# Attention heads in a four-layer network: one pool of six PSUM banks for both score products and the values, and masked scores written in place

## The chip, the cores and the metric

One core of a Trainium2 chip runs the whole program. The metric is the device time of one execution in microseconds, here the median of three runs. The core has a matrix engine (PE, with its weight loads shown as PEld), a vector engine (DVE), an activation engine (ACT), a general engine (POOL) and the queue that issues the DMA transfers (SP). Each engine works through its own instructions in program order, and semaphores hold it where it needs another engine's result. PE writes its products to PSUM, which this kernel uses as eight banks of 512 float32 columns on 128 partitions.

## The reference

The input is x, 2048 rows of 640 values. Four layers follow, attention, Fourier, attention, Fourier, each adding to x:

```python
def _A_ref(x, wqkv, wo):
    H = 32; Dh = D // H; W = 256
    qkv = (lambda x, *d: x.transpose(*d))((x @ wqkv).reshape(B, S, 3, H, Dh), 2, 0, 3, 1, 4)
    q, k, v = qkv[0], qkv[1], qkv[2]
    scores = jnp.einsum("bhqd,bhkd->bhqk", q, k) * (Dh ** -0.5)
    mask = (idx[:, None] - idx[None, :] >= 0) & (idx[:, None] - idx[None, :] < W)
    p = _softmax(jnp.where(mask[None, None], scores, -1e9), axis=-1)
    o = jnp.einsum("bhqk,bhkd->bhqd", p, v)
    return (lambda x, *d: x.transpose(*d))(o, 0, 2, 1, 3).reshape(B, S, D) @ wo
...
x = x + _A_ref(_layernorm(x, axis=-1), A_wqkv, A_wo)
x = x + _B_ref(_layernorm(x, axis=-1), B_dft_seq_re, B_dft_seq_im, B_dft_hid_re, B_dft_hid_im)
x = x + _A_ref(_layernorm(x, axis=-1), A_wqkv, A_wo)
x = x + _B_ref(_layernorm(x, axis=-1), B_dft_seq_re, B_dft_seq_im, B_dft_hid_re, B_dft_hid_im)
```

Each of the 32 heads has 20 values a row, and a row sees itself and the 255 rows before it. `_B_ref` is the real part of a two-dimensional Fourier transform, done as products with given matrices; the change doesn't touch it.

## The kernel before

Products of float32 values are made of three products each: an operand is split into a high and a low part (`split`), and high x high, high x low and low x high are summed. The scores put the three side by side along the 60 rows of one matmul.

In an attention layer the heads are taken four at a time, eight groups called quads, with 16 blocks of 128 rows each. `heads` runs over 128 steps, one for each block of each quad, after ten steps of lead. A step t does several things that belong to different blocks, in two halves z = 0 and z = 1 with two heads each:

- `t_pair` (L571): the transposed scores of block t, keys on the partitions, up to 384 query columns, for two heads into two banks. The heads lie on different rows of PE, so the two matmuls run side by side. `t_exp` (L580) takes both banks through the exponential on ACT in one instruction of 768 columns and writes them to SBUF (`pt`). `t_mask` (L586, L590) clears on POOL what the window leaves out.
- `s_head` (L542, L547): the scores of block t + 10, queries on the partitions, for the row maxima. After the matmul one DVE instruction adds the mask and takes the maximum over each row. It writes the masked scores, which nobody reads, to one scratch tile `ux`, and the maximum to a column of `mc`. A second DVE instruction reads the accumulator out.
- `m_rows` (L555, L558): every fourth step, 16 columns of maxima are transposed on PE, negated on ACT and sent by DMA to a row of `qp`, where the transposed score product takes them up as its 61st row.
- `pv` (L605): at the end of the step, the values of block t - 1: for up to three key blocks, four heads on four column groups of PE, 24 matmuls in all (each float32 product is two). Four blocks share one bank, which `finish` (L617) copies out on ACT as 512 columns. The first row of each head is the sum of the exponentials; its reciprocal (L625) and the values go to DRAM.
- `fill`: between the halves, PE gets other products. For most of a layer these are projections of queries and keys for later quads (`pieces`, run by `lockstep`, L188), about four pairs of matmuls a step; later the first part of the output product (`partials`), nine pairs a step. `lockstep` runs two products side by side on the two halves of PE's rows, first one half of the rows, then, with the halves swapped, the other. Their results are copied out by ACT (L472), POOL (L473, L474) and DVE (L864) when `heavy` is relieved, which is once after each exponential and after some fills.

Which bank a product takes is given by roles: transposed scores banks 0 and 1, scores 2, 3 and 4 in turn, values 5, projections and output 6 and 7.

```python
ROLES = {
    "t": (0, 1), "s": (2, 3, 4), "pv": (5,), "m": (6, 7), "f": (6, 7, 5, 1), "w": (2, 3, 4, 7), "mx": (0,),
```

The matmul that takes a bank waits until the engine that read the bank's former content has done so. The order of all work is fixed in the program: within a step, for each half, transposed scores, scores, transpose of maxima, exponential, masks, one relieved copy, values (second half), fill (first half), then a `tick` that issues the work posted for this half-step.

## Time and profile before

| | us |
|---|---|
| median of 3 runs | 2257.56 |
| lowest and highest run | 2252.48, 2261.92 |
| span of the profiled execution | 2259.9 |
| ACT busy | 1100.4 |
| DVE busy | 1591.1 |
| POOL busy | 1004.5 |

The profiled execution's span runs from its first to its last instruction. No time of its own is given beside it; it lies inside the spread of the three runs. A group row names line, engine, operation, what is written and read, the shape and the count, then the busy time and the mean length of one in ns, then the idle time of the engine just before these instructions and what ended it. Rows of one source line have the shortest, median and longest duration and the first and last start. A timeline row has the start, the length and, in brackets, how long the engine had waited and for whom. Rows of the waits name who waited for whom, then the total in us, the number of times and the longest one.

### The profile page before, as it was taken

Reading aid. Unit: us, or ns where it says so; the run is one execution under the profiler, and the core shown is the slowest. Engines: PE = TensorE matmul, PEld = TensorE weight load, DVE = VectorE, ACT = ScalarE, POOL = GpSimd, SP = SyncE. Lnnn points to the kernel's source line nnn. Section 1 sums busy time; section 2 is a strip of 40 time slices with the busy share of each in tenths; the row PEclk is TensorE's granted clock in tenths of the full one; section 3 lists DMA queues with packets and bytes.
Section 4 is the critical chain, followed back from the end, with each engine's and each line's share of the span. In section 5 each row is a group of like instructions: output and inputs, shape, how many; then the busy total and the mean of one; then the engine's idle time right before and its main releaser. Section 6 shows DMA issues by size and latency. Waiting matters only on the chain.

```text
span 2259.9 us, 49557 instructions
## 1 busy us (share of the span) xinstructions
PE 2164.8 (96%) x17944; PEld 1786.2 (79%) x17944; DVE 1591.1 (70%) x3883; ACT 1100.4 (49%) x1909; POOL 1004.5 (44%) x1534
## 2 busy tenths in 40 slices
PE   7999999899989999999999999999989999999999
PEld 7986666677768888889999766666777688888899
DVE  6347777765888768785661577776758978687766
ACT  2116666655554545452431266666555545455432
POOL 3036666766614132332330466667666132232324
PEclk9999999999999999999999999998999999999999
DMA  5545655774635354656646455566745454537653
GB/s 187 178 149 168 184 172 172 216 211 146 200 117 176 132 172 143 211 180 202 213 141 190 143 181 172 173 192 197 219 145 176 128 174 129 185 124 229 207 177 128
DMA packets 220180, 392.14 MB, mean 174 GB/s; under 512 B 39200, under 2 KB 85792, under 8 KB 219936
## 3 DMA queue, kind: packets, MB, share of 16 engines
q1 hardware_dynamic: 219936, 388.98, 54.7%
q8 instruction: 142, 2.33, 0.4%
q14 instruction: 102, 0.84, 0.1%
HBM read 273.94 MB, written 113.77 MB: 172 GB/s over the span
## 4 chain that ended last, share of the span: by engine, by line
PE 64%; POOL 9%; DMA 7%; ACT 6%; DVE 6%; issue 5%; SPq 3%; ACTq 0%; POOLq 0%; DVEq 0%
PE banks L1245 28%; PE banks L170 13%; PE banks L188 8%; PE banks L1533 5%; PE banks L571 4%; ACT pt L580 3%; PE banks L605 3%; PE banks L542 2%; DMA qp<-qk_d 2%; SPq L505 2%; POOL pt L586 2%; POOL big L163 1%; POOL pt L590 1%; POOL c L474 1%; DVE qp L163 1%
## 5 line engine op out<-in xcount | busy, mean ns | idle before, releaser
L547 DVE CUSTOM_DVE_ANT_0 ux<-banks,mask 128x384 bf16<-128x384 f32 (+2 forms) x1024 | 544.5, 532 | 222.7 <-PE banks L542 106.8
L580 ACT ACTIVATE pt<-banks 128x768 f32<-128x768 f32 (+2 forms) x512 | 394.8, 771 | 308.3 <-PE banks L571 153.3
L586 POOL TENSOR_SCALAR_AFFINE_SELECT pt<-pt 128x256 f32<-128x256 f32 x512 | 209.0, 409 | 242.5 <-ACT pt L580 236.6
L188 PE MATMUL banks<-big,wc 64*128 64x512 f32 x1920 | 279.0, 395 | 0.4 <-DVE pt L371 0.4
L571 PE MATMUL banks<-qp,kp 61*128 61x384 f32 (+2 forms) x1024 | 231.4, 412 | 37.0 <-ACT pt L580 29.7
L571 PEld LDWEIGHTS banks<-qp,kp 61*128 61x128 f32 x1024 | 111.0, 185 | 153.1 <-ACT pt L580 143.6
L605 PE MATMUL banks<-pt,vq 128*32 128x128 f32 x5760 | 218.5, 280 | 8.0 <-POOL pt L586 7.9
L542 PE MATMUL banks<-kp,qp 60*128 60x384 f32 (+2 forms) x1024 | 208.5, 342 | 5.7 <-DVE mc L547 5.5
L188 PEld LDWEIGHTS banks<-big,wc 64*128 64x128 f32 x1920 | 201.2, 186 | 14.5 <-DVE pt L371 0.5
L605 PEld LDWEIGHTS banks<-pt,vq 128*32 128x32 f32 x5760 | 145.1, 110 | 65.5 <-issue 31.8
L163 DVE TENSOR_TENSOR qp<-pt,qp 128x512 fp32r<-128x512 f32 (+1 forms) x199 | 163.7, 828 | 43.7 <-ACT qp L157 41.7
L157 ACT ACTIVATE qp<-pt 128x512 fp32r<-128x512 f32 (+1 forms) x201 | 123.9, 625 | 135.9 <-DVE pt L1179 53.1
L590 POOL TENSOR_SCALAR_AFFINE_SELECT pt<-pt 128x256 f32<-128x256 f32 x448 | 183.9, 410 | 0.0
L1245 PE MATMUL banks<-qp,big 128*128 128x512 f32 x648 | 154.3, 391 | 3.4 <-POOL big L163 3.1
L1178 POOL TENSOR_TENSOR pt<-pt,pt 128x512 f32<-128x512 f32 x34 | 50.1, 1472 | 237.1 <-DMA pt<-c 186.6
L157 ACT ACTIVATE c<-pt 128x512 fp32r<-128x512 f32 x144 | 89.2, 625 | 126.6 <-POOL pt L1165 56.1
L1245 PEld LDWEIGHTS banks<-qp,big 128*128 128x128 f32 x648 | 120.5, 188 | 29.2 <-POOL big L163 4.0
L542 PEld LDWEIGHTS banks<-kp,qp 60*128 60x128 f32 x1024 | 130.4, 189 | 14.7 <-DVE mc L547 10.0
L163 DVE TENSOR_TENSOR c<-pt,c 128x512 fp32r<-128x512 f32 x142 | 114.3, 806 | 25.2 <-ACT c L157 22.5
L1245 PE MATMUL banks<-qp,xc 128*128 128x512 f32 x480 | 119.9, 397 | 6.6 <-DVE xc L163 3.9
L1245 PEld LDWEIGHTS banks<-qp,xc 128*128 128x128 f32 x480 | 90.8, 190 | 28.6 <-DVE xc L163 6.5
L1245 PE MATMUL banks<-c,big 128*128 128x512 f32 x396 | 97.8, 393 | 3.8 <-POOL c L163 2.1
(241 smaller groups left out, 4411.7 us busy)
## 6 DMA issues: line engine op xcount, KB each, us to landing
pt<-c SPq DMA_DIRECT2D x188, 512.0 KB
qk_d<-c SPq DMA_DIRECT2D x80, 512.0 KB
kp<-qk_d SPq DMA_DIRECT2D x384, 80.0 KB
qp<-qk_d SPq DMA_DIRECT2D x384, 80.0 KB
kp<-u_d SPq DMA_DIRECT2D x32, 640.0 KB
o_d<-ou SPq DMA_DIRECT2D x64, 256.0 KB
x_d<-x SPq DMA_DIRECT2D x48, 320.0 KB
v_d<-pt SPq DMA_DIRECT2D x16, 768.0 KB
```

Source lines behind the costliest of these rows:

```text
L157: nc.scalar.activation(hi, src, AF.Copy, scale=-1.0 if neg else 1.0)
L163: (eng or nc.vector).tensor_tensor(out=lo, in0=src, in1=hi.bitcast(F32), op=OP.subtract)
L170: self.nc.tensor.matmul(p, x, y, start=n == 0, stop=n == last)
L188: self.nc.tensor.matmul(ps[a], x[r], y[r], start=half + i == 0, stop=half == 1 and i == n - 1, skip_group_check=True)
L542: nc.tensor.matmul(p, qp[quad % 2][b:b + 60, z, qb * P:(qb + 1) * P], kp[quad % 2][b:b + 60, z, k0 * P:(qb + 1) * P], start=True, stop=True)
L547: nc.vector.tensor_tensor_reduce(out=self.ux[:, :n * P], in0=p, in1=self.mask[:, 384 - n * P:], scale=1.0, scalar=NEG, op0=OP.add, op1=OP.max,
L571: nc.tensor.matmul(p, kp[quad % 2][b:b + 61, z, kb * P:(kb + 1) * P], qp[quad % 2][b:b + 61, z, kb * P:(kb + n) * P], start=True, stop=True)
L580: nc.scalar.activation(pt[quad, kb][:, 2 * z:2 * z + 2, :n * P], self.banks[:, 0:2, :n * P], AF.Exp, scale=SCALE)
L586: nc.gpsimd.affine_select(out=t[:, :, 0:P], in_=t[:, :, 0:P], pattern=[[0, 2], [1, P]], compare_op=OP.is_ge, fill=0.0, base=0, channel_mul ...
L590: nc.gpsimd.affine_select(out=t[:, :, 256:384], in_=t[:, :, 256:384], pattern=[[0, 2], [-1, P]], compare_op=OP.is_gt, fill=0.0, base=0, ch ...
L605: nc.tensor.matmul(acc[quad, bk][32 * h:32 * h + 32, at:at + P], vq[:, 96 * (kb % 4) + 21 * h:96 * (kb % 4) + 21 * h + 32], t[:, h, (qb - ...
L1245: nc.tensor.matmul(self.banks[:, bk, :], p, b[q], start=start and m == 0, stop=stop and last and m == 2, skip_group_check=True)
```

## The change

Banks 0 to 5 become one pool in the heads (0 to 3 ahead of step -1; 0, 1, 4 and 5 in the last steps, when the output product takes 2 and 3). A small planner holds for each bank the time at which it is expected to come free, on a clock of 2.5 us a step. `borrow` takes the banks that are expected free first; `borrow_pair` does so for two neighbouring banks, which the one exponential of 768 columns needs. Each product has an expected time in the step and an expected time of holding. This sets only which bank is named; the waits for what a bank held are those of the program as before.

The masked scores are written back over the scores in PSUM, and `ux` is gone. The values of each block have a bank of their own and are copied out by ACT at once, 128 columns, in place of one copy of 512 after four blocks; the transposed maxima lie in columns 384 and up of the bank taken for the values. `lockstep` has a new DVE instruction between its two halves, which reads one column of both banks into a small tile `seen`. The roles "f" and "w" name other banks.

```diff
+STEP = 2.5
+AT_T, AT_S, AT_PV = (0.0, 1.28), (0.18, 1.46), 1.7
+HELD_T, HELD_S, HELD_PV = 1.4, (0.96, 1.54), 1.3
 ROLES = {
-    "t": (0, 1), "s": (2, 3, 4), "pv": (5,), "m": (6, 7), "f": (6, 7, 5, 1), "w": (2, 3, 4, 7), "mx": (0,),
+    "m": (6, 7), "f": (6, 7, 4, 5), "w": (6, 7, 2, 3),
...
+    def borrow(self, at, *held):
+        free = self.ring6
+        got = sorted(free, key=lambda b: (free[b], b))[:len(held)]
+        for b, d in zip(got, held):
+            free[b] = max(at, free[b]) + d
+        return got
+    def borrow_pair(self, at, held):
+        free = self.ring6
+        b = min((b for b in free if b + 1 in free),
+                key=lambda b: (max(free[b], free[b + 1], at), -min(free[b], free[b + 1]), b))
+        free[b] = free[b + 1] = max(free[b], free[b + 1], at) + held
+        return b, b + 1
...
                 if half == 0:
+                    a = min(self.bank_of[id(p)][0] for p in ps)
+                    self.nc.vector.tensor_copy(self.seen, self.banks[:, a:a + 2, 0])
                     yield 0
...
             nc.vector.tensor_tensor_reduce(
-                out=self.ux[:, :n * P], in0=p, in1=self.mask[:, 384 - n * P:], scale=1.0, scalar=NEG,
+                out=p, in0=p, in1=self.mask[:, 384 - n * P:], scale=1.0, scalar=NEG,
                 op0=OP.add, op1=OP.max,
...
-        def pv(quad, qb):
+        def pv(quad, qb, bank):
...
-                        acc[quad, bk][32 * h:32 * h + 32, at:at + P],
+                        self.banks[32 * h:32 * h + 32, bank, :P],
...
+            nc.scalar.activation(ous[quad, bk][:, at:at + P], self.banks[:, bank, :P], AF.Copy)
             if qb % 4 == 3:
-                self.heavy.append((ROLES["pv"][0], lambda: finish(quad, bk)))
+                finish(quad, bk)
...
+        self.ring6 = dict.fromkeys((0, 1, 2, 3), -99.0)
         for step in range(-LEAD, steps + 1):
             now[0] = step
+            clock = step * STEP
+            if step == -1:
+                self.ring6.update({4: -99.0, 5: -99.0})
+            if step + LEAD == steps + 1:
+                for b in ROLES["w"]:
+                    self.ring6.pop(b, None)
...
                 if 0 <= t < steps:
-                    t_pair(t // 16, t % 16, z)
+                    banks = self.borrow_pair(clock + AT_T[z], HELD_T)
+                    t_pair(t // 16, t % 16, z, banks)
                 if 0 <= s < steps:
-                    for e in range(2):
-                        s_head(s // 16, s % 16, 2 * z + e, "s")
-                m = m_rows(*rows, self.banks[:, 1, :] if 0 <= t < steps else None) if z and rows else iter(())
+                    for e, b in enumerate(self.borrow(clock + AT_S[z], *HELD_S)):
+                        s_head(s // 16, s % 16, 2 * z + e, b)
+                if z and (rows or 0 <= v < steps):
+                    last, = self.borrow(clock + AT_PV, HELD_PV)
+                m = m_rows(*rows, last) if z and rows else iter(())
                 next(m, None)
                 if 0 <= t < steps:
-                    t_exp(t // 16, t % 16, z)
+                    t_exp(t // 16, t % 16, z, banks)
```

More of the change, by code (lines that the diff above doesn't have):

```diff
@@ L77, in __init__ @@
         self.mask = fixed("mask", 384, BF16)
-        self.ux = fixed("ux", 384, BF16)
         self.ones = const.tile([1, 128], F32, name="ones")
@@ L100, in __init__ @@
         self.held = []
+        self.bank_of = {}
+        self.seen = fixed("seen", 2, F32)
     def slot_tile(self, name, cols, dt):
@@ L125, in bank @@
         self.last_bank = k
-        return self.banks[:rows, k, :n]
+        p = self.banks[:rows, k, :n]
+        self.bank_of[id(p)] = k, p
+        return p
+    def borrow(self, at, *held):
[10 more added lines that the diff above has]
+        return b, b + 1
     def next(self, name):
@@ L535, in heads, with s_head @@
         mc = {}
-        def s_head(quad, qb, h, role):
+        def s_head(quad, qb, h, bank):
             n = min(qb + 1, 3)
@@ L540, in s_head @@
             b, z = 64 * (h % 2), h // 2
-            p = self.bank(role, n * P)
+            p = self.banks[:, bank, :n * P]
             nc.tensor.matmul(
@@ L547, in s_head, with m_rows @@
             nc.vector.tensor_tensor_reduce(
-                out=self.ux[:, :n * P], in0=p, in1=self.mask[:, 384 - n * P:], scale=1.0, scalar=NEG,
+                out=p, in0=p, in1=self.mask[:, 384 - n * P:], scale=1.0, scalar=NEG,
                 op0=OP.add, op1=OP.max,
                 accum_out=mc[quad, qb // 4][:, z, h % 2, qb % 4:qb % 4 + 1])
-        def m_rows(quad, u, full=None):
+        def m_rows(quad, u, bank):
             m = mc.pop((quad, u))
-            p = self.bank("mx", P, 16) if full is None else full[:16, 384:]
+            p = self.banks[:16, bank, 3 * P:]
             nc.tensor.transpose(p, m.rearrange("p z e j -> p (z e j)"), self.ident)
@@ L564, in heads, with t_pair @@
         pt = {}
-        def t_pair(quad, kb, z):
+        def t_pair(quad, kb, z, banks):
             n = min(NB - kb, 3)
@@ L569, in t_pair, with t_exp @@
                 b = 64 * e
-                p = self.bank("t", n * P)
                 nc.tensor.matmul(
-                    p, kp[quad % 2][b:b + 61, z, kb * P:(kb + 1) * P],
+                    self.banks[:, banks[e], :n * P], kp[quad % 2][b:b + 61, z, kb * P:(kb + 1) * P],
                     qp[quad % 2][b:b + 61, z, kb * P:(kb + n) * P], start=True, stop=True)
-        def t_exp(quad, kb, z):
+        def t_exp(quad, kb, z, banks):
             n = min(NB - kb, 3)
+            b0, b1 = banks
             if z == 0:
@@ L592, in t_mask @@
                     compare_op=OP.is_gt, fill=0.0, base=0, channel_multiplier=1)
-        acc = {}
-        def pv(quad, qb):
+        ous = {}
+        def pv(quad, qb, bank):
             bk, at = qb // 4, qb % 4 * P
             if qb % 4 == 0:
-                acc[quad, bk] = self.bank("pv")
+                ous[quad, bk] = self.next("ou")
             for kb in range(max(qb - 2, 0), qb + 1):
@@ L729, in heads @@
                     if 0 <= v < steps:
-                        pv(v // 16, v % 16)
+                        pv(v // 16, v % 16, last)
                     for _ in m:
```

7 lines of the change are left out of this document (3 added, 4 removed).

## The prediction

> **What bounds the kernel now.** I read the page first: the span, then the costliest groups and what ended the idle time before them.
>
> ```profile
> span 2259.9 us, 49557 instructions
> PE 2164.8 (96%) x17944; PEld 1786.2 (79%) x17944; DVE 1591.1 (70%) x3883; ACT 1100.4 (49%) x1909; POOL 1004.5 (44%) x1534
> L571 PEld LDWEIGHTS banks<-qp,kp 61*128 61x128 f32 x1024 | 111.0, 185 | 153.1 <-ACT pt L580 143.6
> ```
>
> PE looks full at 96%, but the ends of matmuls are modelled. The weight loads of the transposed scores (L571) tell more: they stood idle for 153.1 us, 143.6 of it until an exponential (L580) had ended. So I asked when L571 runs (the same line in the first and the second attention layer), and looked at a stretch of regular steps by groups.
>
> ```profile
> L571 PEld LDWEIGHTS banks<-qp,kp x512: 182/183/331, 160.4 to 559.9; 61*128 61x128 f32 x171
> L571 PEld LDWEIGHTS banks<-qp,kp x512: 182/183/327, 1282.5 to 1682.2; 61*128 61x128 f32 x171
> ...
> L571 PE MATMUL banks<-qp,kp 61*128 61x384 f32 (+2 forms) x256 | 57.9, 415 | 6.7 <-ACT pt L580 4.3 <-DMA qp<-qk_d 0.4
> L188 PE MATMUL banks<-big,wc 64*128 64x512 f32 x480 | 72.7, 395 | 0.0
> ...
> L571 PE MATMUL banks<-qp,kp 61*128 61x384 f32 (+2 forms) x88 | 20.3, 396 | 3.2 <-ACT pt L580 3.1
> ```
>
> Each layer spends 400 us on its 128 steps, 3.12 us a step. The x256 row covers 210 to 400 us: four L571 matmuls a step make 64 steps, 190/64 = 2.97 us each. In it 480 projection matmuls run in pairs, 3.75 pairs a step. The x88 row covers 450 to 530 us: 22 steps of 3.64 us, where the output product fills PE. One regular step by the timeline (start, length), with some DVE rows ahead of it:
>
> ```profile
> 332.62 0.56 DVE L547 CUSTOM_DVE_ANT_0 ux<-banks,mask 128x384 bf16<-128x384 f32 x1
> 333.10 0.08 DVE L547 DVE_READ_ACCUMULATOR2_ANT mc<- 128x1 f32 x1
> 333.10 0.25 DVE L625 RECIPROCAL rc<-sm 128x16 f32<-128x16 f32 x1
> 333.24 0.59 PEld L605 LDWEIGHTS banks<-pt,vq 128*32 128x32 f32 x24 [0.26 <-issue]
> 333.34 0.56 DVE L547 CUSTOM_DVE_ANT_0 ux<-banks,mask 128x384 bf16<-128x384 f32 x1
> 333.82 0.08 DVE L547 DVE_READ_ACCUMULATOR2_ANT mc<- 128x1 f32 x1
> 334.05 0.56 DVE L547 CUSTOM_DVE_ANT_0 ux<-banks,mask 128x384 bf16<-128x384 f32 x1
> 334.11 0.19 PEld L571 LDWEIGHTS banks<-qp,kp 61*128 61x128 f32 x2 [0.28 <-ACT pt L580]
> 334.11 0.44 PE L571 MATMUL banks<-qp,kp 61*128 61x384 f32 x2
> 334.39 0.34 PE L542 MATMUL banks<-kp,qp 60*128 60x384 f32 x2
> 334.57 1.10 PE L188 MATMUL banks<-big,wc 64*128 64x512 f32 x8
> 334.68 0.81 ACT L580 ACTIVATE pt<-banks 128x768 f32<-128x768 f32 x1 [0.62 <-PE banks L571]
> 334.77 0.56 DVE L547 CUSTOM_DVE_ANT_0 ux<-banks,mask 128x384 bf16<-128x384 f32 x1 [0.15 <-PE banks L542]
> 335.54 0.18 PEld L571 LDWEIGHTS banks<-qp,kp 61*128 61x128 f32 x2 [0.31 <-ACT pt L580]
> 335.82 0.34 PE L542 MATMUL banks<-kp,qp 60*128 60x384 f32 x2
> 336.10 0.86 PE L605 MATMUL banks<-pt,vq 128*32 128x128 f32 x24
> 336.97 0.44 PE L571 MATMUL banks<-qp,kp 61*128 61x384 f32 x2
> ...
> 462.35 0.49 PE L571 MATMUL banks<-qp,kp 61*128 61x384 f32 x2
> 462.53 0.48 PE L542 MATMUL banks<-kp,qp 60*128 60x384 f32 x2
> ```
>
> The L571 pair starts at 334.11, 335.54 and 336.97, every 1.43 us whatever stands between (four projection pairs, or the values). That is one turn of two banks: product 0.44, exponential from 334.68 to 335.49, release 0.05. With banks 0 and 1 alone, a step cannot be under 2 x 1.43 = 2.86; the other 0.11 of 2.97 is what copies on ACT, POOL and DMA add.
>
> A second limit lies just under it. Masked maxima follow one another every 0.71 us (333.34 to 334.05), though a read of the accumulator ends at 333.90: the next waits 0.15. The reciprocal at 333.10 fits into that hole free of cost (332.62 to 333.34 is 0.72), so DVE isn't busy in it. By the code the wait is for the previous write of the one scratch tile ux. Four make 2.84 us a step. A longer transposed-score turn hides it only just.
>
> **The change part by part.**
>
> *Transposed scores in any free pair of six banks.* It removes the 1.43 us turn. With the expected releases worked through, the regular steps repeat every three: the first t pair takes (2,3), the first scores 4 and 5, the second t pair (0,1), the second scores 4 and 2, the values 3; in the next step the names move on to (4,5), and so on. A pair thus follows an exponential by more than half a step. What is late next is the first t pair of a step: one of its banks held the third score of the step before. The loop, from t at 0: the scores at 0.18 (462.35 to 462.53, where L571 was not held), the projection at 0.36, four pairs at (1.10 - 0.395)/3 = 0.235 make 0.94, so second t pair 1.30, second scores 1.48, their product done 1.82, mask begins 1.86 (334.73 to 334.77), accumulator read 0.56 later, 2.42, and the next weight load about 0.05 after: 2.47 us. PE alone: 1.48, values 0.28 later (335.82 to 336.10), 24 weight loads 0.59, and 0.06 for the turn: 2.41. So PE and this loop replace 2.86 by 2.47.
>
> *Maxima in place.* ux goes, and with it the wait on DVE itself: the spacing falls to between 0.48 (start of the accumulator read, where the reciprocal started) and 0.57 (its end). Four are 2.28 at most. A masked maximum that writes PSUM is in no row; two forms give its pace:
>
> ```profile
> L547 DVE CUSTOM_DVE_ANT_0 ux<-banks,mask 128x384 bf16<-128x384 f32 x896 | 498.8, 557 | 165.7 <-PE banks L542 74.2 <-DVE mc L547 2.5 <-PE banks L188 1.0
> L547 DVE CUSTOM_DVE_ANT_0 ux<-banks,mask 128x128 bf16<-128x128 f32 x64 | 18.6, 291 | 28.0 <-PE banks L542 22.9 <-PE banks L605 0.5
> ```
>
> (557 - 291)/256 = 1.04 ns per column, 158 ns fixed. From below: 557, nothing changes (a lower one is unlikely: it streams the same 384 columns). From above: reading and writing one bank take turns, 158 + 2 x 1.04 x 384 = 957. I take 557: only the destination moves. [...]
>
> *The other engines at 2.6 us.* The rows of the same 64 steps:
>
> ```profile
> L580 ACT ACTIVATE pt<-banks 128x768 f32<-128x768 f32 (+2 forms) x128 | 98.8, 772 | 70.4 <-PE banks L571 33.8 <-PE banks L555 17.1 <-PE banks L542 11.9
> L472 ACT ACTIVATE x<-banks 128x512 f32<-128x512 f32 x16 | 9.5, 595 | 0.1
> L617 ACT ACTIVATE ou<-banks 128x512 f32<-128x512 f32 x16 | 9.5, 592 | 0.0
> L558 ACT ACTIVATE mt<-banks 16x128 fp32r<-16x128 f32 x16 | 4.0, 249 | 0.0
> ...
> L586 POOL TENSOR_SCALAR_AFFINE_SELECT pt<-pt 128x256 f32<-128x256 f32 x128 | 52.3, 408 | 64.0 <-ACT pt L580 61.8 <-PE banks L188 0.8
> L590 POOL TENSOR_SCALAR_AFFINE_SELECT pt<-pt 128x256 f32<-128x256 f32 x112 | 45.8, 409 | 0.0
> L474 POOL TENSOR_TENSOR c<-x,c 128x512 fp32r<-128x512 f32 x16 | 20.8, 1303 | 0.0
> L473 POOL CAST c<-x 128x512 fp32r<-128x512 f32 x16 | 9.8, 611 | 0.0
> ```
>
> *Values block by block.* One 592 ns copy in four steps becomes four copies of 128 columns. The nearest row is the 128-column ACT copy, 249 ns: 4 x 0.25 - 0.59 = 0.41 per four steps, 0.10 a step. ACT then has 98.8 + 9.5 + 4.0 + 64 x 0.25 = 128 us, 2.0 a step, and some 0.2 of gaps: it hides under 2.47. Uncovered it would cost 0.10 x 256 steps = 26 us. Each copy waits at the head of ACT's queue for the values' end (about 2.4 + 0.2); behind it stands the next exponential, which can't start before its own product, 0.57 after the next step's start. So the wait holds up nobody. POOL has 128.4 us and the weight splits, 2.0 to 2.1 a step.
>
> *The read of two columns between halves (seen).* 8 projection chunks x 2 and 16 output tiles make 32 reads a layer. Nearest rows: 0.25 (the reciprocal) and 0.29 (the shortest maximum); 64 x 0.29 = 19 us if nothing hid them. The second half comes a step later on PE, and DVE has 2.47 - 2.28 = 0.19 a step to spare: I take nothing. Behind the read stand the second scores' maxima, whose products come after the same fill anyway.
>
> *Moved roles.* Four banks instead of three for scores ahead of step -1, other banks for the first chunks and the end: no term.
>
> **Sum.** Floor 2.47 plus the same 0.11 to 0.15 of irregular work: 2.60 a step against 2.97, 0.37. Projection lasts 95 steps a layer: by the page's x1920 L188 matmuls, 480 pairs a layer, some 122 of them ahead of step -1 (eight steps of two fills of seven, one of ten), 358/3.75 = 95.
>
> ```profile
> L188 PE MATMUL banks<-big,wc 64*128 64x512 f32 x1920 | 279.0, 395 | 0.4 <-DVE pt L371 0.4
> PEld banks L605 <- POOL pt L586: 7.3, 14, 1.7
> DVE rc L625 <- DMA sm<-ou: 3.0, 1, 3.0
> ```
>
> 2 x 95 x 0.37 = 70. The other 33 steps are longer for DMA and output tiles as well; I give them half of it: 2 x 33 x 0.18 = 12. Faster steps leave POOL and loads less time: the first layer's waits above are 7.3 and 3.0; I add 4 a layer, -8. Total 74. The profiled execution shows no time around its span, which is 2.3 us above the median of the runs and inside their spread; 2259.9 - 74 = 2186, less the 2.3, is 2184.
>
> **Rivals.**
>
> *Weaker: POOL sets the step.* In a step with cast and subtraction between the masks it has 4 x 0.41 + 0.61 + 1.30 = 3.55 us, and the values need its last mask. Beyond 2.97 that is 0.58 now, beyond 2.60 it is 0.95: 0.37 more in 24 of 64 steps (16 subtractions, 8 weight splits), 0.14 a step. The gain is 0.23: 44 + 12 less 8, 2210. For it: 7.3 us of waits already. Against it: masks have a step of slack.
>
> *Stronger: PE alone.* 2.41, irregular work absorbed by the six banks: 0.56 x 190 + 20 = 126, 2131. Against it: three other engines are at 80% or more then.
>
> *No change: DVE keeps 0.71*, because the hole after each accumulator read has another cause than ux, or another dependency of DVE on itself stays. 4 x 0.71 = 2.84 plus 0.09 of irregular work (0.11 now): 2.93, gain 0.04 x 256 = 10, 2247. For it: the hole is the same 0.15 after every maximum. Against it: the reciprocal went into the hole. [...]
>
> *Slower: the maximum in one bank takes turns between read and write.* At 957 ns, read included 0.97, four take 3.88; the 118 steps that have both products, at 3.9 instead of 3.12, are 92 a layer: 2257.6 + 184 = 2442. It decides from a spacing of 2.97/4 = 0.74 on. For it: no row writes PSUM from DVE. Against it: PE adds 512 columns onto a bank in 0.235 us, 0.46 ns a column, by the L188 row, so a bank takes more than one access in 1.04 ns. [...]
>
> **How the numbers follow.** Forecast 0.56, weaker 0.15, stronger 0.08, no change 0.09, slower 0.12. Half a per cent, 11 us, is about what a measurement of this kernel tells from none. Faster 0.79 (the first three), same 0.09, slower 0.12. The range, 2145 to 2250, holds forecast, weaker and no change; the stronger and the slower are the 2 in 10 left out. The forecast's own is 2150 to 2215.
>
> **What would show it.** L571 pairs no longer 1.43 apart, steps of 2.5 to 2.7 in 200 to 360 us; weight-load idle of L571 until L580 near nothing, some of it until the masked maximum instead; maxima 0.48 to 0.6 apart and 557 long; four ACT copies near 250 ns. Wrong would be a maximum above 0.7, a spacing that stays 0.71, or waits of the values on POOL of 20 us and more.

## The result, and the profile after

| | before | after |
|---|---|---|
| median, us | 2259.74 | 2223.82 |
| lowest and highest run, us | 2252.48, 2263.68 | 2223.56, 2225.32 |
| span of the profiled execution, us | 2259.9 | 2222.2 |

The ratio is 0.9841, with a 95% interval of 0.9828 to 0.9855: 36 us faster. Each kernel has four runs here; the median of before ahead of the prediction is of three of them. The forecast was 2184, 74 us. The direction came as predicted and the time lies inside the range given (2145 to 2250), but above the likeliest case's own (2150 to 2215): about half of the forecast gain is missing.

First the page after (the transposed scores are now line 595, the scores 567, the masked maxima 572, the exponential 605, the values 630 and their copy 637).

```profile
span 2222.2 us, 48837 instructions
L572 DVE CUSTOM_DVE_ANT_0 banks<-banks,mask 128x384 f32<-128x384 f32 (+2 forms) x1024 | 528.0, 557 | 150.5 <-PE banks L567 127.9
L595 PEld LDWEIGHTS banks<-qp,kp 61*128 61x128 f32 x1024 | 106.9, 186 | 81.2 <-DVE mc L572 52.0
L637 ACT ACTIVATE ou<-banks 128x128 f32<-128x128 f32 x256 | 71.5, 279 | 87.4 <-PE banks L630 76.7
```

The weight loads of the transposed scores idle 81.2 us in place of 153.1, and no longer until the exponential but mostly until a masked maximum (52.0), as the loop of the prediction wants. The maximum got a little longer: 557 ns is now its mean over all three forms, where before it was 532; the form of 384 columns, 557 before, takes 582 (its row stands in the last section). The block copies cost 279 ns each where 249 was taken, and ACT waits 87.4 us in front of them, so they are covered.

Next the same line in each attention layer: durations, first and last start.

```profile
L595 PEld LDWEIGHTS banks<-qp,kp x512: 182/183/328, 161.6 to 544.0; 61*128 61x128 f32 x171
L595 PEld LDWEIGHTS banks<-qp,kp x512: 182/183/327, 1265.8 to 1644.5; 61*128 61x128 f32 x171
```

The heads take 382.4 and 378.7 us in place of 399.5 and 399.7: 17.1 and 21.0 us gained, 38 together, which is the whole gain (37.7 by the two spans). To see where in a layer, the starts of the transposed scores were counted between 210 and 380 us, where only projections fill. A step has four such loads, in two pairs that start together:

```profile
L571 PEld LDWEIGHTS banks<-qp,kp x228: 182/183/186, 210.2 to 378.8; 61*128 61x128 f32 x114
```

```profile
L595 PEld LDWEIGHTS banks<-qp,kp x246: 182/183/185, 211.0 to 378.5; 61*128 61x128 f32 x123
```

Before (the first row), 228 loads are 114 pairs, 113 half steps in 168.6 us, 2.98 us a step; after, 122 half steps in 167.5 us, 2.75. So 0.24 a step was gained (2.984 less 2.746) where 0.37 was forecast. One regular step of the timeline after, with two maxima of the step ahead:

```profile
302.24 0.57 DVE L572 CUSTOM_DVE_ANT_0 banks<-banks,mask 128x384 f32<-128x384 f32 x1
302.73 0.14 DVE L572 DVE_READ_ACCUMULATOR2_ANT mc<- 128x1 f32 x1
302.73 0.60 DVE L572 CUSTOM_DVE_ANT_0 banks<-banks,mask 128x384 f32<-128x384 f32 x1
302.92 0.19 PEld L595 LDWEIGHTS banks<-qp,kp 61*128 61x128 f32 x2 [0.62 <-DVE mc L572]
303.20 0.36 PE L567 MATMUL banks<-kp,qp 60*128 60x384 f32 x2
303.38 1.11 PE L211 MATMUL banks<-big,wc 64*128 64x512 f32 x8
304.31 0.36 PE L595 MATMUL banks<-qp,kp 61*128 61x384 f32 x2
304.49 0.35 PE L567 MATMUL banks<-kp,qp 60*128 60x384 f32 x2
304.87 0.57 DVE L572 CUSTOM_DVE_ANT_0 banks<-banks,mask 128x384 f32<-128x384 f32 x1
305.35 0.14 DVE L572 DVE_READ_ACCUMULATOR2_ANT mc<- 128x1 f32 x1
305.55 0.19 PEld L595 LDWEIGHTS banks<-qp,kp 61*128 61x128 f32 x2 [0.20 <-DVE mc L572]
```

From 302.92 to 305.55 is a step of 2.63 us, and it is the predicted loop, read along its own rows: first transposed scores to scores 0.28, scores to projection 0.18, four pairs 0.93, second transposed scores to their scores 0.18, to the third maximum 0.38, to its accumulator read 0.48, the read 0.14, to the next load 0.06. The sum is 2.63; the prediction's was 2.47.

### The profile page after: what moved, and what is told of

Its sections match the earlier page's. It is cut to its first block, busy times and chain, and to the rows that moved or that the text cites. A ratio compares the mean times of both kernels' runs of the same rounds, so it can differ in the third digit from the quotient of the medians.

```text
span 2222.2 us, 48837 instructions
## 1 busy us (share of the span) xinstructions
PE 2130.6 (96%) x17944; PEld 1782.5 (80%) x17944; DVE 1603.5 (72%) x3947; ACT 1128.9 (51%) x2101; POOL 1004.8 (45%) x1534
## 4 chain that ended last, share of the span: by engine, by line
PE 71%; POOL 8%; DVE 8%; DMA 4%; issue 4%; ACT 4%; SPq 1%; POOLq 0%; ACTq 0%; DVEq 0%
PE banks L1280 27%; PE banks L193 14%; PE banks L211 10%; PE banks L630 6%; PE banks L1568 5%; PE banks L595 4%; PE banks L567 4%; POOL pt L611 2%; POOL pt L615 1%; POOL c L499 1%; POOL big L186 1%; ACT pt L605 1%; DVE qp L186 1%; DVE banks L572 1%; DMA vq<-v_d 1%
## 5 line engine op out<-in xcount | busy, mean ns | idle before, releaser
L572 DVE CUSTOM_DVE_ANT_0 banks<-banks,mask 128x384 f32<-128x384 f32 (+2 forms) x1024 | 528.0, 557 | 150.5 <-PE banks L567 127.9
L611 POOL TENSOR_SCALAR_AFFINE_SELECT pt<-pt 128x256 f32<-128x256 f32 x512 | 210.5, 412 | 205.3 <-ACT pt L605 187.1
L211 PE MATMUL banks<-big,wc 64*128 64x512 f32 x1920 | 269.8, 395 | 0.4 <-DVE pt L396 0.4
L595 PE MATMUL banks<-qp,kp 61*128 61x384 f32 (+2 forms) x1024 | 208.2, 382 | 17.0 <-DVE mc L572 12.3
L567 PE MATMUL banks<-kp,qp 60*128 60x384 f32 (+2 forms) x1024 | 201.5, 347 | 12.9 <-DVE mc L572 10.8
L186 DVE TENSOR_TENSOR qp<-pt,qp 128x512 fp32r<-128x512 f32 (+1 forms) x209 | 178.7, 858 | 38.8 <-ACT qp L180 37.6
L211 PEld LDWEIGHTS banks<-big,wc 64*128 64x128 f32 x1920 | 185.1, 186 | 24.3 <-ACT x L497 1.8
L180 ACT ACTIVATE qp<-pt 128x512 fp32r<-128x512 f32 (+1 forms) x209 | 129.1, 624 | 118.6 <-DVE pt L1214 54.7
L615 POOL TENSOR_SCALAR_AFFINE_SELECT pt<-pt 128x256 f32<-128x256 f32 x448 | 184.6, 412 | 0.0
L595 PEld LDWEIGHTS banks<-qp,kp 61*128 61x128 f32 x1024 | 106.9, 186 | 81.2 <-DVE mc L572 52.0
L567 PEld LDWEIGHTS banks<-kp,qp 60*128 60x128 f32 x1024 | 122.2, 188 | 36.7 <-DVE mc L572 22.5
L572 DVE DVE_READ_ACCUMULATOR2_ANT mc<- 128x1 f32 x1024 | 145.5, 142 | 0.0
L637 ACT ACTIVATE ou<-banks 128x128 f32<-128x128 f32 x256 | 71.5, 279 | 87.4 <-PE banks L630 76.7
```

The lines of the kernel that those rows point to most:

```text
L180: nc.scalar.activation(hi, src, AF.Copy, scale=-1.0 if neg else 1.0)
L186: (eng or nc.vector).tensor_tensor(out=lo, in0=src, in1=hi.bitcast(F32), op=OP.subtract)
L211: self.nc.tensor.matmul(ps[a], x[r], y[r], start=half + i == 0, stop=half == 1 and i == n - 1, skip_group_check=True)
L567: nc.tensor.matmul(p, qp[quad % 2][b:b + 60, z, qb * P:(qb + 1) * P], kp[quad % 2][b:b + 60, z, k0 * P:(qb + 1) * P], start=True, stop=True)
L572: nc.vector.tensor_tensor_reduce(out=p, in0=p, in1=self.mask[:, 384 - n * P:], scale=1.0, scalar=NEG, op0=OP.add, op1=OP.max, accum_out=mc ...
L595: nc.tensor.matmul(self.banks[:, banks[e], :n * P], kp[quad % 2][b:b + 61, z, kb * P:(kb + 1) * P], qp[quad % 2][b:b + 61, z, kb * P:(kb + ...
```

## The experiments

One table of all runs: the mean step from the same count of loads (last start less first start, over a quarter of the loads less two), the median and the ratio to before. Each is the changed kernel with the edit shown, except b_inplace, which is the kernel before with an edit. Each ratio is to runs of the kernel before from the same session; their median was 2256.7 to 2259.7, so the ratios compare better than the medians.

| label | loads, first to last start | step, us | median, us | ratio, 95% interval |
|---|---|---|---|---|
| before | 228, 210.2 to 378.8 | 2.98 | 2259.74 | 1 |
| after | 246, 211.0 to 378.5 | 2.75 | 2223.82 | 0.9841, 0.9828 to 0.9855 |
| a_ux | 238, 210.8 to 379.5 | 2.86 | 2241.11 | 0.9930, 0.9915 to 0.9945 |
| b_inplace | 228, 210.5 to 378.9 | 2.98 | 2260.19 | 1.0008, 0.9990 to 1.0026 |
| k_five | 234, 210.4 to 379.9 | 2.92 | 2254.62 | 0.9991, 0.9982 to 1.0000 |
| c_max256 | 248, 210.9 to 378.9 | 2.73 | 2219.42 | 0.9835, 0.9819 to 0.9852 |
| h_pv2 | 254, 210.7 to 379.2 | 2.67 | 2211.48 | 0.9794, 0.9775 to 0.9812 |
| i_both | 258, 210.6 to 379.3 | 2.64 | 2201.51 | 0.9750, 0.9724 to 0.9775 |
| f_pool | 254, 210.0 to 379.6 | 2.69 | 2214.13 | 0.9809, 0.9785 to 0.9832 |
| m_wc | 252, 210.2 to 378.7 | 2.70 | 2242.13 | 0.9922, 0.9905 to 0.9938 |
| e_recip | 246, 210.7 to 379.4 | 2.77 | 2217.57 | 0.9826, 0.9811 to 0.9840 |
| r_late | 248, 210.1 to 379.0 | 2.75 | 2241.65 | 0.9923, 0.9902 to 0.9944 |
| l_best1 | 248, 211.0 to 378.4 | 2.72 | 2232.26 | 0.9886, 0.9868 to 0.9903 |
| n_best2 | 218, 210.6 to 378.8 | 3.11 | 2306.51 | 1.0221, 1.0192 to 1.0250 |
| q_best3 | 248, 210.5 to 378.6 | 2.73 | 2210.92 | 0.9786, 0.9771 to 0.9802 |

### Which part of the change carries the gain

**a_ux**: the scratch tile comes back (the read between the halves writes to it too), all else as changed.

```diff
-                out=p, in0=p, in1=self.mask[:, 384 - n * P:], scale=1.0, scalar=NEG,
+                out=self.ux[:, :n * P], in0=p, in1=self.mask[:, 384 - n * P:], scale=1.0, scalar=NEG,
```

> The changed kernel with the masked scores going to the scratch tile ux again (the read between the halves writes there too). Theory 1, that each masked maximum then waits for the one before it: spacing 0.71 us, accumulator read 82 ns, so four fill 2.84 us and the regular step goes from 2.62 back to 2.84 or a little more; 88 steps in two layers lose 0.22 each, 2224 + 39 = 2263. Theory 2, that the pool of banks alone carries the gain and DVE was never a bound: regular steps stay at 2.62 and the time at 2224 (within 8).

The timeline of this run:

```profile
332.27 0.56 DVE L572 CUSTOM_DVE_ANT_0 ux<-banks,mask 128x384 bf16<-128x384 f32 x1
332.76 0.08 DVE L572 DVE_READ_ACCUMULATOR2_ANT mc<- 128x1 f32 x1
332.99 0.56 DVE L572 CUSTOM_DVE_ANT_0 ux<-banks,mask 128x384 bf16<-128x384 f32 x1
...
335.12 0.56 DVE L572 CUSTOM_DVE_ANT_0 ux<-banks,mask 128x384 bf16<-128x384 f32 x1
```

The read ends at 332.84 and the next maximum starts at 332.99, 0.15 later; the first to the fifth maximum, 332.27 to 335.12, is 2.85, the vector engine's own floor of 4 x 0.71. The step is as expected. The total is not as long as expected (2263), because the mean is no longer than this floor (2.86): by the starts of the loads, two of the longer steps of every 16 go down to 2.84 (from 2.89 and 2.85), and four others stay at 2.59 to 2.72. That DVE waits for its own write fits the traces too: the line of the maxima has 1022 semaphore instructions of DVE before, 40 after. The place that the masked scores go to came back together with the wait, so a scratch tile without a wait (two in turn) remains untried.

**b_inplace**: the kernel before, with the masked scores in place and nothing else.

```diff
-                out=self.ux[:, :n * P], in0=p, in1=self.mask[:, 384 - n * P:], scale=1.0, scalar=NEG,
+                out=p, in0=p, in1=self.mask[:, 384 - n * P:], scale=1.0, scalar=NEG,
```

> The kernel before with the masked scores written in place and nothing else changed. Theory 1, that the turn of the two banks 0 and 1 (product, exponential, release) is the first bound: regular steps stay at 2.86 and the time within 10 us of 2259.7. Theory 2, that the wait of DVE on itself was the bound: steps of 2.7 or less, and 2235 or less.

The step stays 2.98 and the ratio's interval holds 1. By its code DVE has no scratch tile left to wait for, and the loads and products of the transposed scores still stand idle for exponentials, 186.6 us in all (173.3 before). So with banks 0 and 1 alone the turn of 1.43 us holds the step though DVE is freed, as the prediction had read it.

**k_five**: the values go to bank 5 as before the change, four blocks in one bank and one copy of 512 columns; the pool has five banks, and the transposed maxima lie in the bank of the second transposed pair.

```diff
-                        self.banks[32 * h:32 * h + 32, bank, :P],
+                        self.banks[32 * h:32 * h + 32, 5, at:at + P],
...
-            nc.scalar.activation(ous[quad, bk][:, at:at + P], self.banks[:, bank, :P], AF.Copy)
             if qb % 4 == 3:
+                nc.scalar.activation(ous[quad, bk], self.banks[:, 5, :], AF.Copy)
...
-                self.ring6.update({4: -99.0, 5: -99.0})
+                self.ring6.update({4: -99.0})
```

> The changed kernel with the values as before: bank 5 for four blocks, one copy of 512 columns, and a pool of five banks for the two score products (transposed maxima in the spare columns of the second transposed pair's bank). Theory: the sixth bank and the copies block by block matter, because five banks leave 0.5 of a bank to spare; the next pair then often waits for the fourth maximum instead of the third, 0.49 to 0.56 us later: regular steps of 2.75 to 3.0, 2240 to 2262. Rival: five banks do as well and save the copies on ACT, 2224 or less.

The step is 2.92 and the time that of before, to 0.1%. A pool with in-place maxima but one bank less gains next to nothing: the sixth bank, together with the block-by-block copies that set it free, carries 2254.62 - 2223.82 = 31 us. The planner's times were those for six banks, so a plan made for five might lose less. The three parts don't add up, each is worth something only where the others have moved their bound.

### What sets the regular step at 2.63

The loop through the third maximum measures 2.63. But PE's own stream could be as long: with no other engine in it, it was put at 2.41. Two kernels shorten one of them each, a third both.

**c_max256**: the maxima run over the last 256 columns only, so the row maximum leaves the oldest key block out.

```diff
-                out=p, in0=p, in1=self.mask[:, 384 - n * P:], scale=1.0, scalar=NEG,
+                out=p[:, max(n - 2, 0) * P:], in0=p[:, max(n - 2, 0) * P:], in1=self.mask[:, 384 - min(n, 2) * P:], scale=1.0, scalar=NEG,
```

> The changed kernel with the maxima taken over the last 256 of 384 columns: the first third of the masked scores takes no part in the maximum. Each masked maximum is 0.13 us shorter. Theory 1, that the regular step of 2.62 is the loop first transposed pair, scores, fill, second scores, third maximum, next first pair: the regular step falls by 0.13 to about 2.49, and 88 steps in two layers give 23, so 2201. Theory 2, that PE's own stream is the bound at 2.62: no change of the step, 2224 within 6.

**h_pv2**: the values of two key blocks in place of three, 16 matmuls.

```diff
-            for kb in range(max(qb - 2, 0), qb + 1):
+            for kb in range(max(qb - 1, 0), qb + 1):
```

> The changed kernel with the values of two key blocks at most (the third, the oldest, is left out): 16 matmuls of the values a step instead of 24, 0.2 us of PE less. Theory 1, that the loop through the third maximum holds the regular step at 2.62 by itself: regular steps stay at 2.62. Theory 2, that PE's own stream is the only bound: regular steps fall by 0.2 to 2.43, and the time by 0.2 x 176 = 35. Theory 3, that both lie within 0.03 of one another: the step stays at 2.62 here, and falls only in the next kernel.

**i_both**: both edits.

> Both at once: maxima over the last 256 columns (the first third takes no part) and values of two key blocks at most (the oldest left out). Theory 3, that loop and PE stream are two bounds at 2.62 and 2.65: regular steps fall to 2.45 to 2.50, the mean of steps 16 to 80 to about 2.58, the time to 2224 - 0.16 x 176 = 2196. Theory 4, that a third thing (ACT's exponential and value copy, or POOL) holds the step: it stays above 2.58.

The timeline of c_max256 in a step with all 24 matmuls of the values:

```profile
340.44 0.19 PEld L595 LDWEIGHTS banks<-qp,kp 61*128 61x128 f32 x2 [0.20 <-DVE mc L572]
340.73 0.34 PE L567 MATMUL banks<-kp,qp 60*128 60x384 f32 x2
340.90 1.09 PE L211 MATMUL banks<-big,wc 64*128 64x512 f32 x8
341.83 0.36 PE L595 MATMUL banks<-qp,kp 61*128 61x384 f32 x2
342.00 0.37 PE L567 MATMUL banks<-kp,qp 60*128 60x384 f32 x2
342.30 0.60 PEld L630 LDWEIGHTS banks<-pt,vq 128*32 128x32 f32 x24 [0.19 <-issue]
342.37 0.43 DVE L572 CUSTOM_DVE_ANT_0 banks<-banks,mask 128x256 f32<-128x256 f32 x1 [0.40 <-PE banks L567]
342.72 0.46 DVE L572 CUSTOM_DVE_ANT_0 banks<-banks,mask 128x256 f32<-128x256 f32 x1
343.09 0.19 PEld L595 LDWEIGHTS banks<-qp,kp 61*128 61x128 f32 x2 [0.20 <-DVE mc L572]
```

The third maximum (342.37) is over early: the fourth begins at 342.72 together with the third's read, which needs 0.14, so that is done at 342.86. The next load begins only at 343.09, though the row names the maximum; it begins 0.19 after the last load of the values (342.30 + 0.60). The step is still 2.65. Here it is PE alone: 0.29 + 0.17 + 0.93 + 0.17 + 0.30 + 0.60 + 0.19. With h_pv2 the loop stays and a step is 2.63 (341.67 to 344.30 below). With both edits it falls to 2.50 and 2.52 (333.45, 335.95, 338.47):

```profile
341.67 0.19 PEld L595 LDWEIGHTS banks<-qp,kp 61*128 61x128 f32 x2 [0.62 <-DVE mc L572]
344.30 0.19 PEld L595 LDWEIGHTS banks<-qp,kp 61*128 61x128 f32 x2 [0.20 <-DVE mc L572]
```

```profile
333.45 0.19 PEld L595 LDWEIGHTS banks<-qp,kp 61*128 61x128 f32 x2 [0.27 <-DVE mc L572]
335.95 0.19 PEld L595 LDWEIGHTS banks<-qp,kp 61*128 61x128 f32 x2 [0.26 <-DVE mc L572]
338.47 0.19 PEld L595 LDWEIGHTS banks<-qp,kp 61*128 61x128 f32 x2 [0.48 <-DVE mc L572]
```

So neither reading alone holds: two bounds lie within 0.03 us of one another, and taking one away shows the other. The mean of h_pv2 fell by 0.07 all the same, by other steps: of every 16, five of the six that take 2.61 to 2.65 in the kernel after stay at 2.61 to 2.62, while the seventh, eighth and eleventh (2.68, 2.59 and 2.95) fall by 0.21 each, about the time of the eight loads of the values that are left out. PE's stream sets those. The mean step of i_both (2.64) fell a little less than its regular one, because the irregular steps don't follow in full.

### What the irregular steps are

In the timeline after, the step that takes longest has these rows on POOL and PE:

```profile
267.72 1.03 POOL L186 TENSOR_TENSOR wc<-x,wc 128x384 fp32r<-128x384 f32 x1
268.71 1.29 POOL L499 TENSOR_TENSOR c<-x,c 128x512 fp32r<-128x512 f32 x1
269.96 0.40 POOL L611 TENSOR_SCALAR_AFFINE_SELECT pt<-pt 128x256 f32<-128x256 f32 x1
270.41 0.14 PEld L630 LDWEIGHTS banks<-pt,vq 128*32 128x32 f32 x4 [0.87 <-POOL pt L611]
```

A split of projection weights (1.03) and the subtraction of a copy (1.29) stand ahead of a mask, and the last four loads of the values wait for it. Two kernels take one of the two sides away.

**f_pool**: the mask for keys further back than the window (L615) is left out, so keys outside the window enter.

```diff
-            if n == 3:
+            if False:
```

> The changed kernel without the second mask on POOL (the far edge of the window is not cleared, so the exponentials there stay): 56 mask instructions of 0.41 us less in 32 steps, 0.7 us of POOL a step. Theory 1, that regular steps are set by the loop through the third maximum and the irregular 0.12 a step above it by casts and subtractions on POOL ahead of the masks: regular steps stay at 2.62, the mean of steps 16 to 80 falls from 2.74 to about 2.65, the time by 0.09 x 176 = 16 to 2208. Theory 2, that POOL has nothing to do with it: mean 2.74, 2224 within 6. Theory 3, that POOL sets the regular steps too: 2.62 falls below 2.55.

**m_wc**: the weight splits are posted six half-steps later.

```diff
-                self.post(3 * i, lambda ks=ks: self.split(w[:, 0, ks], w[:, 1, ks], raw[:, ks], eng=self.nc.gpsimd))
+                self.post(6 + 3 * i, lambda ks=ks: self.split(w[:, 0, ks], w[:, 1, ks], raw[:, ks], eng=self.nc.gpsimd))
```

> The changed kernel with the weight splits of the next projection chunk issued six half-steps later, so that POOL no longer has them together with the subtractions of a finished piece. Theory 1, that the one step of 3.59 in sixteen comes from POOL doing a weight split (1.03) and a subtraction (1.29) ahead of the masks that the values wait for: that step falls to 2.9 or less, the mean of steps 16 to 80 from 2.74 to 2.70, the time by 0.045 x 176 = 8, to 2216. Theory 2, that the work only meets the masks elsewhere: another step gets longer by as much, the mean stays 2.74, the time 2224 within 4.

Both bring the mean step down (2.69 and 2.70 from 2.75), f_pool less than expected (2.65). By the starts of the loads it is this one step in 16: 3.58 after, 2.84 in f_pool, 2.63 in m_wc, where the two steps behind it grow together by 0.34. The four other long steps, 2.85 to 2.95, stay as they are in both; each holds a transpose of maxima or a subtraction, and no run takes these away. So this collision is about half of the irregular 0.12, and the other half stays open. And m_wc lost more than it gained ahead of the heads. This row of the lead was in it:

```profile
PEld banks L211 <- POOL wc L186: 11.7, 2, 6.2
```

The first chunks of the projections need their split weights at once, so the first transposed scores start at 178.6 instead of 161.6 us. The price of a later split is paid where nothing else covers it.

### Why the late steps gained nothing

In the last steps of a layer the output product takes the place of the projections, from 432 us on in the first. Just ahead of it these rows stand in the timeline after, and a row of the windows (a stretch, its length, the busy times of PE, PEld, DVE, ACT and POOL, then the granted clock, 0.51):

```profile
422.03 0.25 DVE L650 RECIPROCAL rc<-sm 128x16 f32<-128x16 f32 x1 [1.87 <-DMA sm<-ou]
422.85 0.44 PE L567 MATMUL banks<-kp,qp 60*128 60x384 f32 x2 [1.84 <-DVE mc L572]
426.06 1.51 PE L630 MATMUL banks<-pt,vq 128*32 128x128 f32 x24
```

```profile
425.00:432.00 7.00, 6.14 (x61) 3.91 (x61) 4.24 (x16) 3.39 (x8) 7.00 (x11) 0.51 0.83 274
```

A reciprocal waits for its sums from DRAM; the maxima queue behind it, PE idles 1.84 us, and some 3 us later 24 matmuls of the values take 1.51 us where they took 0.86 at 423.22 (the granted clock from 420 to 424 us was 1.00). The reciprocals' waits make 7.1 us in this layer, 3.0 before.

**e_recip**: the reciprocals and what follows them are posted three half-steps later.

```diff
-            at = (2, 7, 9) if quad < NQ - 1 else (1, 5, 6)
+            at = (2, 10, 12) if quad < NQ - 1 else (1, 7, 8)
```

> The changed kernel with the reciprocals issued three half-steps later and their stores with them (10 and 12 half-steps behind the values instead of 7 and 9; in the last quad 7 and 8 instead of 5 and 6). Theory 1, that the last 39 steps of a layer gained nothing because DVE, in order, waits at reciprocals for the load of the sums, PE stops behind it and its clock is then halved for a while: the waits of 7.1 us at reciprocals in the first layer go, the half-clock stretches of 10.2 and 3.4 us there go or shorten, and the time falls by 8 to 16, to about 2212. Theory 2, that the loads of the output product set these steps: steps 88 to 127 stay at 129 to 133 us and the time at 2224 within 5.

The heads take 378.3 us (160.9 to 539.2) and 378.2 (1260.1 to 1638.3): 4.1 and 0.5 less. The waits of reciprocals on a DMA are gone from the list, and the clock stays whole in the stretch where it was halved:

```profile
425.00:432.00 7.00, 6.22 (x97) 4.21 (x97) 6.10 (x23) 3.52 (x10) 6.68 (x13) 1.00 0.89 271
```

In the same 7 us PE runs 97 matmuls instead of 61. Most of it is given back soon: a pair of transposed scores now waits 2.75 us for a row of maxima that comes by DMA, and 2.4 us later such a pair takes 0.78 us in place of 0.45.

```profile
440.23 0.45 PE L595 MATMUL banks<-qp,kp 61*128 61x384 f32 x2 [2.75 <-DMA qp<-mt]
442.59 0.78 PE L595 MATMUL banks<-qp,kp 61*128 61x384 f32 x2
```

The total, 2217.57, is 6 us under that of the change by the medians and 3 us by the ratios, whose intervals overlap: a gain is likely but not clear, and it is less than the 8 to 16 us expected.

**r_late**: six pairs of the output product a step in place of nine; the rest runs after the heads. Its output is no longer the reference's, and its total (2241.65) is above the 2215 to 2230 expected, which wasn't followed up; only the steps are read.

```diff
-LATE = 9
+LATE = 6
```

> Six pairs of the output product a step in the late steps in place of nine; what is left of it runs after the heads. Theory (PE's own stream is the bound of the late steps: nine pairs of 320 columns, loads and turns): steps 104 to 112 fall from 3.4 us to 2.8 to 2.95. Rival (the waits on DMA, the masks on POOL and the output adds on DVE set the late steps): they stay at 3.2 to 3.4 us. The total stays at 2215 to 2230 by both, since the left-out pairs are made up after the heads.

Eight late steps and the first pair of the next (34 loads) in the kernel before, in the kernel after and in this one:

```profile
L571 PEld LDWEIGHTS banks<-qp,kp x34: 182/183/185, 481.9 to 509.4; 61*128 61x128 f32 x34
```

```profile
L595 PEld LDWEIGHTS banks<-qp,kp x34: 182/183/184, 466.4 to 493.5; 61*128 61x128 f32 x34
```

```profile
L595 PEld LDWEIGHTS banks<-qp,kp x34: 182/183/185, 461.0 to 482.6; 61*128 61x128 f32 x34
```

Eight steps are 27.5 us before, 27.1 after and 21.6 here: 3.44, 3.39 and 2.70 us a step. Three pairs less take 0.69 us off each step, more than expected, which is back at the length of the regular ones. So the output product's own work, on PE and in the additions on DVE that come with it, fills the late steps (the two weren't told apart); the masks and the transfers of the heads, which are the same in r_late, don't set them. And they had been as long before the change: in these 27.5 us the transposed scores' loads waited 3.7 us for exponentials, so the faster turn of the banks had little to free there.

### Versions built on what was found

**l_best1**: e_recip and m_wc together.

> The changed kernel with both: reciprocals three half-steps later (2217.6 alone) and weight splits six half-steps later. If both are independent, 2217.6 - 8 = 2210; if the second only moves its stall, 2217.

**n_best2**: the same, and a quarter of the projections' fill moved between the second scores and the values.

```diff
+                    if -1 <= t < steps:
+                        fill(nf / 4)
                     if 0 <= v < steps:
                         pv(v // 16, v % 16, last)
...
-                    fill(nf)
+                    fill(nf * 3 / 4 if -1 <= t < steps else nf)
```

> The kernel with both delays, and one of about four projection pairs a step moved from between the halves to between the second scores and the values. The third maximum then begins 0.235 us earlier in the step. Theory 1, that loop and PE's stream are two bounds within 0.03: regular steps with 24 value matmuls stay at 2.62 to 2.65, those with 8 or 16 fall to about 2.5, 3 of 16 steps, so 0.02 a step and 4 us, 2206. Theory 2, that the loop alone is the bound: all regular steps fall to 2.45, and the time by 25.

l_best1 has the shortest heads of the kernels that leave nothing out (370.7 us, 174.3 to 545.0; 372.6, 1280.2 to 1652.8) and much of m_wc's loss ahead of them, so that its 2232.26 us misses both of the times expected. n_best2 is slower than before, where 2206 was expected; its waits from 162 to 545 us have these rows:

```profile
PEld banks L630 <- issue: 30.1, 107, 0.5
PEld banks L595 <- issue: 19.2, 91, 0.4
PEld banks L211 <- ACT x L497: 10.7, 12, 1.0
```

In the kernel after they are 18.4, 6.3 and 0.8. The fill now meets a bank that ACT has yet to copy out, and each step has one more change between kinds of matmul. These rows are 34 us longer. The granted clock may have a part in it too: over the whole profiled execution its mean is 0.986, where it is 0.993 in the kernel after. What each of them costs wasn't tried.

**q_best3**: e_recip, and the weight splits later only after the lead.

```diff
-                self.post(3 * i, lambda ks=ks: self.split(w[:, 0, ks], w[:, 1, ks], raw[:, ks], eng=self.nc.gpsimd))
+                self.post(3 * i + (0 if self.lead else 6), lambda ks=ks: self.split(w[:, 0, ks], w[:, 1, ks], raw[:, ks], eng=self.nc.gpsimd))
```

> The reciprocals three half-steps later, and the weight splits on POOL six half-steps later, but only after the lead. Theory (the loss of the former two runs was the lead, whose projections waited for their weights; in the steps the collision with the masks goes away): the first transposed-score pair is back at 161 to 163 us, the heads after it take 368 to 371 us a layer, so about 10 us a layer less than with the late reciprocals alone is not reached but 5 to 6 us is: 2217.6 - 11 = 2206. Rival (the moved splits cost elsewhere in the steps what they free between the masks): 2217, heads 373 to 377 us.

The first transposed scores start at 160.0 us again, and the heads take 375.1 us (160.0 to 535.1) and 375.4 (1256.0 to 1631.4), about 3 us a layer less than e_recip. The gain on e_recip is 6.7 us where 11 were expected, and the length of the heads is the one that the rival gave (373 to 377): the step of 3.55 falls to 2.63, but the two behind it grow together by about 0.4. It is the fastest of the versions that leave nothing out: 2210.92 us, ratio 0.9786, interval 0.9771 to 0.9802, 13 us under the changed kernel.

## Why the prediction was right in its steps and wrong in its size

**The turn of two banks** held: with the old banks a faster DVE changes nothing (b_inplace), and with the pool the 1.43 us spacing is gone.

**The maxima in place** held: the spacing went from 0.71 to 0.49 (302.24 to 302.73), and with the scratch tile back the step is 2.85 (a_ux). The scratch tile, with the wait for it, makes the spacing 0.22 us longer, and with the pool it costs 17 us in all (2241.11 less 2223.82). The rival of an unchanged spacing of 0.71 fell, and so did the one of a maximum of 957 ns: it takes 582 where 557 was taken.

**The step that failed is the floor of the sum, sized at 2.47 from the loop and 2.41 from PE alone.** Both are 2.63 to 2.65, so the stronger rival, with 2.41, was out of reach as well. Over the 190 projection steps that the prediction counted, 0.16 a step is 30 us; with the 12 us of the late steps that is 42, and the gain fell short by 38. Three things were missing in the floor. The first transposed scores to the scores took 0.28 and not 0.18: I used a row of a load that wasn't held, but behind the values this pair always starts afresh, so 0.10 goes into both bounds. The accumulator read after an in-place maximum takes 142 ns and not 82, which makes the way from the mask's start to the next load's bank 0.62 instead of 0.56: 0.06 into the loop. And PE's stream back from the values to the transposed scores takes 0.20 instead of 0.06: 0.14 into PE alone. 2.47 + 0.16 = 2.63, 2.41 + 0.24 = 2.65. The prediction's own rows had the sign of it, a load of the values that idled 0.26 with no releaser but "issue". The waits after show it as a cost of its own:

```profile
PEld banks L630 <- issue: 18.4, 86, 0.3
PEld banks L595 <- issue: 6.3, 30, 0.4
```

0.21 us each time, before the values and after. In 60 of the 64 steps from the 17th on, the first load of the transposed scores stood idle for 0.20, whoever is named; in the other four it waited longer, for a maximum. These are the places where PE goes from two tiles of rows to four of columns and back. No run takes this change alone away, so that it is the cause is my inference from the places and not shown; that PE alone needs 2.65 is shown by c_max256.

**The 0.11 to 0.15 of irregular work** held (2.75 - 2.63 = 0.12), and its longest step was the one that the weaker rival named, POOL's splits and subtractions ahead of a mask (f_pool, m_wc). That rival had its price right, 0.95 beyond a regular step (3.58 less 2.63; 0.61 before, 3.47 less 2.86), but not its count: it is one step in 16, not 24 in 64. Its time, 2210, came closest of all cases, and that was luck: the irregular part didn't grow, the floor did. (POOL's four rows add up to 128.7 us, not 128.4, which changes nothing.)

**The late steps**, taken at half of the gain (12 us), gave about nothing, because the output product's work fills them (r_late). This was to be read before: the x88 row's steps of 3.64 us are far above two turns of 1.43. And faster steps led the reciprocals into waits (7.1 us, 3.0 before) and PE into a granted clock of 0.51 from 425 to 432 us (1.00 there in e_recip), for which 4 us a layer had been taken off.

**Beside the path**, as forecast: the values' copies (279 ns each), and the moved roles (the first transposed scores start at 161.6 us, 160.4 before). Whether the read between the halves is as free as taken stays open: the steps that hold one are among the shortest (2.59 and 2.43), but they have three pairs of projections and not four, and a kernel without the read wasn't tried.

## What to carry to other kernels

When a bound is taken away, build the next one from rows that stand in the same place of the sequence: here the first transposed scores, behind the values, took 0.28 us to the next product and the second ones, behind the projection, 0.18, and 0.1 us in a loop of 250 turns was a third of the gain forecast. List every bound that lies within a tenth of the new floor, because taking one away buys only the distance to the next; and ask of each stretch whether it has that bound at all before giving it a share of the gain. Work that is moved later for the sake of the steady part must be left alone in the lead, where nothing covers it.

## What the runs showed of the hardware

In the step shown of the kernel after, the masked maximum that waited for nothing started with the accumulator read of the one before it, at 302.73, 0.49 us after that maximum, which took 0.57, had started. Writing float32 over its own input in PSUM, in place of bfloat16 to SBUF, made the 384-column form a little longer, not twice as long, and the read after it too (142 ns, 82 before):

```profile
L572 DVE CUSTOM_DVE_ANT_0 banks<-banks,mask 128x384 f32<-128x384 f32 x896 | 484.3, 582 | 110.3 <-PE banks L567 89.3 <-PE banks L595 5.4
L572 DVE DVE_READ_ACCUMULATOR2_ANT mc<- 128x1 f32 x1024 | 145.5, 142 | 0.0
```

582 ns in place of 557. And a pause of 1.84 us on PE was followed, some 2 us after its end, by a granted clock of 0.51 over the 7 us shown; from 420 to 424 us, where the pause lay, PE was busy for 2.16 of the 4 us and the clock was still 1.00. In e_recip, where no reciprocal waits for a DMA, the clock in the same 7 us was 1.00. How long a pause it takes is not shown by these runs.
